# Loading three of four blocks of the near values again, in three transfers

## The chip, the cores and the metric

The kernel runs on one core of a Trainium2 chip. The metric is the device time of one execution in microseconds (us), the median of several runs.

## The reference, cut to what matters

```python
B, H, S, D = 4, 8, 768, 64             # block = 32, so 24 blocks of rows
scores = matmul(q, k.T) / sqrt(D)
mask = |blk_i - blk_j| <= 1            # neighbours
mask |= blk_i in (0, 23) or blk_j in (0, 23)     # end rows, end columns
mask |= blk_j in sampled_blocks[blk_i]           # three sampled blocks a row block
attn = softmax(where(mask, scores, -1e9))
x = matmul(attn, v)                    # (B, S, 512) after the heads are joined
# channel mix of x, shifted by one row
xk = mu_k * x + (1 - mu_k) * x_prev
xr = mu_r * x + (1 - mu_r) * x_prev
out = sigmoid(xr @ w_r) * (relu(xk @ w_k) ** 2 @ w_v)
```

A row block in the middle of a sequence sees eight key blocks: three sampled ones, its own with the two neighbours, and the two end blocks 0 and 23.

## The kernel before, in words

**Units.** The attention is done in 24 units: for each pair of batches one wide unit (the two end row blocks, which see all keys) and eleven near units of two neighbouring row blocks each (`UNITS`). Near unit m of a pair covers row blocks n = 2m+1 and n+1 for both batches, all eight heads. The matmuls of the channel mix are laid between those of the attention as their rows come ready.

**Buffers of near values.** For each of its two row blocks (j = 0, 1) a near unit needs two value buffers of 128 partitions by 4 KB (512 KB): one for the "far" side and one for the "near" side, each with four blocks of 32 rows. Partition k\*4+n holds row k of block n. The near side of j = 0 holds blocks [23, n-1, n, n+1], that of j = 1 holds [n, n+1, n+2, 23], so block 23 stands in the first place for j = 0 and in the last for j = 1, whatever the unit. The far side holds the three sampled blocks and block 0. There are eight buffers `VR[0..7]`: the first and second near units take four each, and from the third on `place_value` hands out `VR[0..3]` in turn, the same four for every unit: `VR[0]` and `VR[2]` for the far side, `VR[1]` and `VR[3]` for the near side. So a unit's values can be loaded only when the unit before has computed its value product.

**Loading.** `load_near` adds the loads of a unit to the plan. `close` (the near side) is one transfer of 512 KB of `vn`, in which the host has laid the four blocks in order. `gather` (the far side) is one transfer of 128 KB of `vt` for each sampled block, whose place is read from a register; block 0 is loaded only when the buffer doesn't hold it already (`slots` remembers for which pair it does). The keys of the near blocks come from `kd` (line 394) into the one key buffer `KR`, the queries from `qn` (line 379).

**Order.** All these transfers are issued by SP, one after the other. The order of all operations on every engine is written out by hand in `ORDER`; the numbers count the operations as they were added to the plan. `Plan.order` also bounds the bytes under way: an operation with transfers waits for the landing of the one that lies `QUEUED` = 2.2 million bytes back, counted with `wire` (bytes and a share for each row) by transfer (`parts` of an operation).

**What reads them.** `near_unit` computes scores (line 553; in the first three near units line 509) from `KR` and the queries, and the value product (line 583) from all four buffers of the unit: 128 matmuls in two groups of 64. The channel mix follows with r (line 773), h (line 793) and v (line 819). Its shifted and mixed inputs xk and xr are made in `split_x` (lines 739 to 752).

Of the kernel before, what the change touches and what calls it, by code (L numbers as in the profile page):

```python
# [25 lines left out]
QB, SLOTS = (4, 8)  # L26
# [4 lines left out]
SEEN = 5  # L31
DIRECT = 3
NEARBY = 0
COPIED = 4
FAR = 8000000000.0
ROOM = 32
# [4 lines left out]
def wire(size, row):  # L41
    return size * (1 + 195 / row)
# [109 lines left out]
def chosen(kind, i):  # L152
    return LETTER[PICK[kind][i]]
# [6 lines left out]
def block_sparse_attention_channel_mix(ctx: ExitStack, tc: tile.TileContext, kt, kd, kw, qw, qn, vt, vn, vw, blocks, own_near, mu_k, mu_r, w_k, w_v, w_r, out):  # L160
    nc = tc.nc
# [3 lines left out]
    plan = Plan()  # L165
    unit = WIDE_SCALE
    PE, ACT, DVE, POOL, SP = ('PE', 'ACT', 'DVE', 'POOL', 'SP')

    def buf(shape, dtype, tag, bufs, name, pool=sb):
        return Buf(pool, shape, dtype, tag, bufs, name)  # L170

    def fixed(shape, dtype, name):
        return Fixed(cp.tile(shape, dtype, name=name))

    def engine(on):
        return nc.scalar if on == ACT else nc.gpsimd if on == POOL else nc.vector

    def copy(on, to, of):
        if on == ACT:
            nc.scalar.copy(to, of)  # L180
        else:
            engine(on).tensor_copy(to, of)  # L182
# [6 lines left out]
    VR = [fixed([P, PAIR, DM], F32, f'VR{i}') for i in range(VR_BUFS)]  # L189
# [114 lines left out]
    slots = [None] * len(VR)  # L304
    turns = [0, 0]

    def place_value(kind):
        turns[kind] += 1
        first = len(VR) // 2
        return 2 * (turns[kind] - 1 if turns[kind] <= first else (turns[kind] - 1 - first) % (VR_BUFS // 2)) + kind  # L310

    def sampled_block(eng, pr, m, i):
        j, i = divmod(i, NRAND)
        n = PAIR * m + 1 + j
        if (eng.engine, n) not in sampled:
            _, (sampled[eng.engine, n],) = nc.values_load_multi_w_load_instructions(packed.ap[0:1, n:n + 1], engines=[eng.engine], min_val=0, max_val=ROOM ** NRAND - ROOM ** (NRAND - 1) * (ROOM - NB) - 1, skip_runtime_bounds_check_because='VectorE keeps each number within the blocks')
        if (eng.engine, pr, n, i) in sampled:
            return sampled[eng.engine, pr, n, i]
        at = sampled[eng.engine, n] >> 5 * i
        if i < NRAND - 1:  # L320
            kept = eng.alloc_register(f'block{pr}_{n}_{i}')
            eng.reg_alu(kept, at, ROOM - 1, ALU.bitwise_and)
            at = eng.snap(kept, min_val=0, max_val=NB - 1)
        else:
            at = nc.s_assert_within(at, 0, NB - 1, skip_runtime_bounds_check_because='VectorE keeps each number within the blocks')
        sampled[eng.engine, pr, n, i] = at
        return at
# [46 lines left out]
    def direct(pr, m):  # L374
        return pr == 0 and m < DIRECT

    def load_near(pr, m, i):
        q = buf([P, HP, P], F32, 'q', 2, f'q{pr}_{m}')
        plan.add(SP, lambda: nc.sync.dma_start(q.ap, qn[pr, m]), writes=[(q, *range(HP))], size=wire(262144, 2048))
        values = []  # L380
        n = PAIR * m + 1
        K = KR
        all_keys = whole[pr]
        by_block = lambda: all_keys.ap.rearrange('p h b (n x) -> p (h b) n x', x=BLK)
        if not m:

            def ends():
                for slot, end in ((END, 0), (WINDOW - 1, NB - 1), (2 * END + 1, 0), (WINDOW + 4, NB - 1)):
                    copy(POOL, K.ap[:, slot], by_block()[:, :, end])
            plan.add(POOL, ends, reads=[(all_keys, *EVERY)], writes=[(K, 'ends')])  # L390
        if pr == 0 and m < COPIED:
            plan.pick('near', m, lambda: copy(chosen('near', m), K.ap[:, WINDOW:WINDOW + 4], by_block()[:, :, n - 1:n + 3].rearrange('p a n x -> p n a x')), reads=[(all_keys, *EVERY)], writes=[(K, 'near')])
        else:
            plan.add(SP, lambda: nc.sync.dma_start(K.ap[:, WINDOW:WINDOW + 4].rearrange('p n a x -> p (n a x)'), kd[pr, :, n - 1:n + 3].rearrange('p n x -> p (n x)')), writes=[(K, 'near')], size=wire(524288, 4096))
        for j in range(PAIR if i in SENT else 0):

            def send(j=j):
                for r in range(NRAND):
                    at = sampled_block(nc.sync, pr, m, j * NRAND + r) + pr * NB
                    nc.sync.dma_start(K.ap[:, (NRAND + 1) * j + r].rearrange('p a x -> p (a x)'), kt[bass.ds(at, 1)].rearrange('o p x -> (o p) x'))  # L400
            plan.add(SP, send, reads=[(packed,)], writes=[(K, ('far', j))], size=wire(131072, 1024) * NRAND, parts=NRAND)
        for j in range(0 if i in SENT else PAIR):

            def fetch(j=j, key=PAIR * i + j):
                on = chosen('keys', key)
                eng = engine(on)
                for i in range(NRAND):
                    at = sampled_block(eng, pr, m, j * NRAND + i)
                    copy(on, K.ap[:, (NRAND + 1) * j + i], by_block()[:, :, bass.ds(at, 1)].rearrange('p a o x -> p a (o x)'))
            plan.pick('keys', PAIR * i + j, fetch, reads=[(packed,), (all_keys, *EVERY)], writes=[(K, ('far', j))])  # L410
        for j in range(PAIR):
            w = [place_value(0), place_value(1)]
            values.append(w)
            more = slots[w[0]] != pr
            slots[w[0]] = pr
            slots[w[1]] = None

            def close(w=w, j=j):
                nc.sync.dma_start(VR[w[1]].ap.rearrange('p b x -> p (b x)'), vn[pr, m, j])

            def gather(w=w, j=j, more=more):
                to = VR[w[0]].ap.rearrange('(k n) b x -> k n (b x)', n=QB)
                if more:
                    nc.sync.dma_start(to[:, NRAND], vt[pr * NB].rearrange('k b x -> k (b x)'))
                for i in range(NRAND):
                    nc.sync.dma_start(to[:, i], vt[bass.ds(sampled_block(nc.sync, pr, m, j * NRAND + i) + pr * NB, 1)].rearrange('o k b x -> (o k) (b x)'))  # L426
            plan.add(SP, close, writes=[(VR[w[1]], 0, 1)], size=wire(524288, 4096))
            plan.add(SP, gather, reads=[(packed,)], writes=[(VR[w[0]], 0, 1)], size=wire(131072, 4096) * (NRAND + more), parts=NRAND + more)
        return (q, K, values)

# [38 lines left out]
    def eight(keys, half, hp, j):  # L469
        i, b = (j % PAIR, j // PAIR)  # L470
        x = keys.ap[half, (NRAND + 1) * i:(NRAND + 2) * i + 1, PAIR * hp + b]
        block = PAIR * HP * BLK
        apart = (WINDOW - 1 + 2 * i - (NRAND + 1) * i) * block
        return replace(x, ap=[list(x.ap[0]), [apart, 2], [block, QB], [1, BLK]])
# [21 lines left out]
    def first_scores(pr, m, gi, s, q, keys):  # L496

        def mm():
# [3 lines left out]
            for a in range(2):  # L502
                hp = 2 * gi + a
                for j in range(QB):
                    i, b = (j % PAIR, j // PAIR)
                    for row, half in enumerate(HALF):
                        to = s.ap[ROWS[j], row, a * 256:(a + 1) * 256].rearrange('p (x r) -> p r x', r=SLOTS)
                        if not NEARBY:
                            nc.tensor.matmul(s.ap[ROWS[j], row, a * 256:(a + 1) * 256].rearrange('p (x g a) -> p g a x', g=2, a=QB), q.ap[half, hp, ROWS[j]], eight(keys, half, hp, j), start=False, stop=True, skip_group_check=True)
# [29 lines left out]
    def near_unit(b, m, together, carried, q, keys, values, o, L, t0, t1):  # L539
        scores, held = ([], [])  # L540
        for gi in range(2):
            s = buf([P, 2, 512], F32, 's', 2, f's{b}_{m}_{gi}', ps)
            if direct(b, m):
                plan.add(PE, first_scores(b, m, gi, s, q, keys), reads=[(q, 2 * gi, 2 * gi + 1), (keys, 'ends', ('far', 0), ('far', 1), *(() if NEARBY else ('near',))), (ident_16,), (first_mask,)] + [(whole[b], *EVERY)] * NEARBY, writes=[(s,)])
                scores.append(s)
# [350 lines left out]
    for op in plan.order():  # L896
        done = nc.cur_bb.bb.instructions
        n = len(done)
# [196 lines left out]
```

## Time and profile before

| | us |
|---|---|
| median of three runs | 527.81 |
| lowest and highest run | 527.33 and 532.04 |
| the profiled execution, its own time | 525.43 |
| its span (first to last instruction) | 523.7 |
| TensorE (PE) busy in the span | 506.4 |

Times in the rows below are microseconds from the start of the span. PE is TensorE's matmul, DVE VectorE, ACT ScalarE, POOL GpSimd; SP issues transfers, and "SPq" marks the issue of a transfer, not its flight. In the timeline a row is: start, time that it took, engine, line, operation, out<-in, count (a run of equal instructions is merged), and in brackets the engine's idle time before it and what ended it. The granted clock of TensorE is full in all 40 slices of the span.

### The profile page before, as it was taken

The numbers are of one execution on the slowest core, as the hardware profiler recorded it, in microseconds if no ns is written. First come the engines' busy times: TensorE is split into PE (matmuls) and PEld (weight loads), VectorE is DVE, ScalarE is ACT, GpSimd is POOL, SyncE is SP. The second block draws the span as 40 slices with busy tenths as digits, with TensorE's granted clock in tenths as the row PEclk, the third lists the DMA queues.
The fourth block names the chain that finished last, engine by engine and source line by source line (L and its number), as shares of the span: only waits on it lengthen the run. The fifth ranks groups of instructions, "written<-read, shape, count | busy, mean of one in ns | idle before, by whom it ended". The sixth has DMA issues, their size and how long they took to land.

```text
span 523.7 us, 17903 instructions
## 1 busy us (share of the span) xinstructions
PE 506.4 (97%) x7026; PEld 404.5 (77%) x7031; DVE 347.0 (66%) x841; ACT 309.1 (59%) x779; POOL 223.8 (43%) x288
## 2 busy tenths in 40 slices
PE   7889799999999999999999999999999999999997
PEld 2456578778878787677887888888988788888886
DVE  5899799986575775557767687675787536426401
ACT  2979898868746664365666467455675355343320
POOL 0634464433443635254063642353363444724530
PEclk9999999999999999999999999999999999999999
DMA  8999894663688887768977876877757414001002
GB/s 293 401 324 342 303 315 169 205 201 102 183 282 242 285 306 202 222 192 265 293 243 206 242 243 182 274 245 209 226 167 213 147 48 110 1 21 60 1 0 80
DMA packets 51765, 105.34 MB, mean 201 GB/s; under 512 B 7329, under 2 KB 27938, under 8 KB 51682
## 3 DMA queue, kind: packets, MB, share of 16 engines
q1 hardware_dynamic: 51394, 103.82, 62.3%
q8 instruction: 55, 0.90, 0.7%
q10 hardware_dynamic: 288, 0.39, 0.2%
q14 instruction: 28, 0.23, 0.1%
HBM read 80.07 MB, written 6.29 MB: 165 GB/s over the span
## 4 chain that ended last, share of the span: by engine, by line
PE 85%; DMA 7%; SPq 3%; DVE 3%; issue 1%; ACT 1%; ACTq 0%; DVEq 0%
PE v L819 25%; PE o L583 8%; PE s L553 7%; PE r_0p L773 5%; PE r_1p L773 5%; PE h_3p L793 5%; PE h_1p L793 4%; PE h_2p L793 4%; PE h_0p L793 4%; PE tx L643 2%; SPq L426 2%; DMA raw<-w_v 1%; PE sw L599 1%; PE t L461 1%; PE h_0p L805 1%
## 5 line engine op out<-in xcount | busy, mean ns | idle before, releaser
L819 PE MATMUL v<-w,k 128*128 128x512 f32 (+1 forms) x600 | 143.5, 390 | 0.0
L819 PEld LDWEIGHTS v<-w,k 128*128 128x128 f32 x600 | 107.8, 188 | 25.8 <-issue 1.4
L447 DVE CUSTOM_DVE_ANT_1 p<-s,near_mask 128x256 f32<-128x256 f32 x152 | 82.9, 628 | 27.4 <-DMA p<-tb 14.0
L452 ACT ACTIVATE p<-p,nm 128x256 f32<-128x256 f32 x152 | 76.1, 502 | 38.1 <-DVE nm L447 35.6
L182 POOL COPY KR<-keys 128x256 f32 (+2 forms) x72 | 30.3, 460 | 44.4 <-PE s L553 21.9
L479 DVE STREAM_TRANSPOSE tb<-p 128x1024 f32<-128x1024 f32 x30 | 37.2, 1240 | 12.4 <-ACT p L452 10.3
L822 DVE SCALAR_TENSOR_TENSOR z<-v,z 128x512 f32<-128x512 f32 (+1 forms) x25 | 16.4, 664 | 39.1 <-PE v L819 38.9
L553 PE MATMUL s<-KR,q 64*32 64x256 f32 x1216 | 38.7, 380 | 1.5 <-issue 1.4
L583 PEld LDWEIGHTS o<-VR,p 128*32 128x32 f32 x1920 | 28.0, 110 | 5.9 <-issue 3.3
L583 PE MATMUL o<-VR,p 128*32 128x64 f32 x1920 | 30.5, 220 | 0.8 <-PE r_0p L773 0.6
L553 PEld LDWEIGHTS s<-KR,q 64*32 64x32 f32 x1216 | 21.2, 106 | 12.7 <-issue 2.9
L773 PE MATMUL r_1p<-w,xr 128*128 128x512 f32 x120 | 30.3, 399 | 0.0
L773 PE MATMUL r_0p<-w,xr 128*128 128x512 f32 x120 | 30.2, 398 | 0.0
L452 ACT ACTIVATION_READ_ACCUMULATOR p<-p,nm 128x1 f32 x152 | 28.7, 189 | 0.0
L773 PEld LDWEIGHTS r_1p<-w,xr 128*128 128x128 f32 x120 | 22.1, 188 | 5.8 <-ACT xt L679 0.4
L773 PEld LDWEIGHTS r_0p<-w,xr 128*128 128x128 f32 x120 | 21.9, 188 | 4.7
L793 PE MATMUL h_3p<-xk,w 128*128 128x256 f32 x192 | 25.2, 285 | 0.0
L452 ACT ACTIVATE pw<-pw,nmw 128x768 f32<-128x768 f32 x16 | 14.9, 935 | 17.4 <-DVE nmw L447 10.0
L793 PE MATMUL h_2p<-xk,w 128*128 128x256 f32 x192 | 24.8, 285 | 0.0
L793 PEld LDWEIGHTS h_3p<-xk,w 128*128 128x128 f32 x192 | 23.5, 188 | 1.4 <-issue 0.8
L793 PEld LDWEIGHTS h_1p<-xk,w 128*128 128x128 f32 x192 | 23.3, 188 | 1.6 <-ACT pt L180 0.4
L793 PE MATMUL h_1p<-xk,w 128*128 128x256 f32 x192 | 24.4, 283 | 0.0
(226 smaller groups left out, 1048.0 us busy)
## 6 DMA issues: line engine op xcount, KB each, us to landing
VR<-vn SPq DMA_DIRECT2D x42, 512.0 KB, 4.9
VR<-vt SPq DMA_DIRECT2D x130, 128.0 KB, 3.3
p<-tb SPq DMA_DIRECT2D x120, 128.0 KB, 2.9
KR<-kd SPq DMA_DIRECT2D x18, 512.0 KB, 4.8
out<-z SPq DMA_DIRECT2D x23, 256.0 KB, 2.8
q<-qn SPq DMA_DIRECT2D x22, 256.0 KB, 5.2
keys<-kw SPq DMA_DIRECT2D x7, 768.0 KB, 7.5
raw<-w_k SPq DMA_DIRECT2D x4, 1024.0 KB, 8.0
```

Of the source, the lines that this page charges most:

```text
L182: engine(on).tensor_copy(to, of)
L426: nc.sync.dma_start(to[:, i], vt[bass.ds(sampled_block(nc.sync, pr, m, j * NRAND + i) + pr * NB, 1)].rearrange('o k b x -> (o k) (b x)'))
L447: nc.vector.tensor_tensor_reduce(out=dealt(p.ap[:, cs]), in0=cut(view()), in1=by, scale=-SCALE, scalar=3e+38 if first is None else nm.ap[: ...
L452: plan.add(ACT, lambda: nc.scalar.activation(p.ap[:, cs], p.ap[:, cs], AF.Exp, bias=nm.ap[:, col:col + 1], scale=-1.0, accum_out=L.ap[:, h ...
L479: plan.add(DVE, lambda: nc.vector.transpose(out=turned.ap.rearrange('p (k y c) -> p k y c', k=QB, c=BLK), in_=p.ap.rearrange('p (y k c) -> ...
L553: nc.tensor.matmul(s.ap[ROWS[j], row, a * 256:(a + 1) * 256].rearrange('p (x g a) -> p g a x' if carried else 'p (x a g) -> p g a x', g=2, ...
L583: nc.tensor.matmul(o.ap[ROWS[j], h * D:(h + 1) * D], held[gi][1](i, g, j), VR[values[j % PAIR][g]].ap[:, j // PAIR, h * D:(h + 1) * D], st ...
L643: nc.tensor.transpose(tp.ap[:, c, :], x.ap[:, c * P:(c + 1) * P], ident.ap)
L773: nc.tensor.matmul(pr.ap[:, 0:512], xr.ap[:, a, c, :], wr[c].ap[:, w, :], start=c == 0 and m == 0, stop=c == CC - 1 and m == 2)
L793: nc.tensor.matmul(ph.ap[:, ff * PAIR * TT:(ff + 1) * PAIR * TT], wk[f // 4 * CC + c].ap[:, w, f % 4 * P:(f % 4 + 1) * P], xk.ap[:, a, c, ...
L819: nc.tensor.matmul(pv.ap[:, 0:width], hid[f][2](a), wv[f].ap[:, w, cs], start=f == 0 and m == 0, stop=f == FC - 1 and m == 2)
L822: plan.add(DVE, lambda pv=pv, cs=cs: nc.vector.scalar_tensor_tensor(out=z.ap[:, cs], in0=pv.ap[:, 0:width], scalar=unit, in1=z.ap[:, cs], ...
```

## The change

For the third to seventh near unit of the first pair of batches (positions 3 to 7 in `UNITS`, below `ENDS_KEPT` = 8) `close` no longer loads block 23, which an earlier unit of the same pair has left in the same place of the same buffer. The other three blocks come as three transfers of 128 KB, each to every fourth partition, instead of one of 512 KB. `slots` now remembers for a near-side buffer the pair and j whose end block it holds. The counts for `QUEUED` follow. `ORDER` is the same; `close` stays one operation with three transfers issued one after another. The values that reach the product are the same.

```diff
+ENDS_KEPT = 8
...
             slots[w[0]] = pr
-            slots[w[1]] = None
-
-            def close(w=w, j=j):
-                nc.sync.dma_start(VR[w[1]].ap.rearrange('p b x -> p (b x)'), vn[pr, m, j])
+            kept = slots[w[1]] == (pr, j) and i < ENDS_KEPT
+            slots[w[1]] = (pr, j)
+
+            def close(w=w, j=j, kept=kept):
+                if not kept:
+                    nc.sync.dma_start(VR[w[1]].ap.rearrange('p b x -> p (b x)'), vn[pr, m, j])
+                    return
+                by_block = lambda x: x.rearrange('(k n) x -> k n x', n=QB)
+                for n in range(1 - j, QB - j):
+                    nc.sync.dma_start(by_block(VR[w[1]].ap.rearrange('p b x -> p (b x)'))[:, n], by_block(vn[pr, m, j])[:, n])
...
-            plan.add(SP, close, writes=[(VR[w[1]], 0, 1)], size=wire(524288, 4096))
+            plan.add(SP, close, writes=[(VR[w[1]], 0, 1)], size=wire(131072, 4096) * (QB - 1) if kept else wire(524288, 4096), parts=QB - 1 if kept else 1)
```

## Rows read from the trace of the kernel before

**Rows 1.** The page, part 4: the chain that ended last, by engine.

```profile
PE 85%; DMA 7%; SPq 3%; DVE 3%; issue 1%; ACT 1%; ACTq 0%; DVEq 0%
```

**Rows 2.** PE's waits: in total, times, longest (us).

```profile
PE o L583 <- DMA VR<-vn: 1.2, 1, 1.2
```

**Rows 3.** The chain that ended last, from 20 to 160: start, us.

```profile
63.63 5.67 DMA VR<-vn
```

**Rows 4.** Timeline of PE, 20 to 170.

```profile
69.35 1.88 PE L583 MATMUL o<-VR,pt 128*32 128x64 f32 x120 [1.23 <-DMA VR<-vn]
...
72.01 3.08 PE L793 MATMUL h_0p<-xk,w 128*128 128x256 f32 x24
...
75.45 1.09 PE L553 MATMUL s<-KR,q 64*32 64x256 f32 x32
...
83.99 1.10 PE L583 MATMUL o<-VR,pt 128*32 128x64 f32 x64
...
101.86 1.10 PE L583 MATMUL o<-VR,pt 128*32 128x64 f32 x64
102.89 1.09 PE L553 MATMUL s<-KR,q 64*32 64x256 f32 x32
...
118.04 1.10 PE L583 MATMUL o<-VR,pt 128*32 128x64 f32 x64
...
139.12 1.99 PE L583 MATMUL o<-VR,pt 128*32 128x64 f32 x128
```

**Rows 5.** Timeline of SP's issues, 20 to 170.

```profile
58.27 5.31 SPq L426 DMA_DIRECT2D VR<-vt  x6
63.63 1.10 SPq L419 DMA_DIRECT2D VR<-vn  x1
...
65.93 0.33 SPq L394 DMA_DIRECT2D KR<-kd  x1
...
75.51 1.99 SPq L426 DMA_DIRECT2D VR<-vt  x3
...
89.78 0.33 SPq L419 DMA_DIRECT2D VR<-vn  x1
...
92.78 5.00 SPq L426 DMA_DIRECT2D VR<-vt  x6
97.88 0.53 SPq L394 DMA_DIRECT2D KR<-kd  x1
...
111.22 1.98 SPq L426 DMA_DIRECT2D VR<-vt  x3
...
133.95 0.53 SPq L419 DMA_DIRECT2D VR<-vn  x1
134.57 0.38 SPq L823 DMA_DIRECT2D out<-z  x1
137.46 2.61 SPq L483 DMA_DIRECT2D p<-tb  x4
```

**Rows 6.** Line 426's instructions from 58.2 to 63.5: landing of its six transfers.

```profile
DMA to landing us min/median/max: 3.3/5.0/6.6
```

**Rows 7.** Timeline of POOL, 55 to 104.

```profile
69.84 1.30 POOL L752 TENSOR_TENSOR xk<-xk_0f,xk 128x512 fp32r<-128x512 f32 x1 [0.82 <-DVE xk L182]
```

**Rows 8.** Transfers issued at 65.93: count, size, us from issue to landing.

```profile
KR<-kd SPq DMA_DIRECT2D x1, 512.0 KB, 9.1
```

**Rows 9.** Line 424's instructions: time of an issue, ns, min/median/max.

```profile
L424 SPq DMA_DIRECT2D VR<-vt x4: 497/548/793, 25.3 to 241.0; - x4
```

**Rows 10.** SP's waits, 58 to 136.

```profile
SPq L419 <- PE o L583: 21.5, 4, 8.1
```

**Rows 11.** The transfer issued at 97.29.

```profile
VR<-vt SPq DMA_DIRECT2D x1, 128.0 KB, 2.5
```

**Rows 12.** The transfer issued at 97.88.

```profile
KR<-kd SPq DMA_DIRECT2D x1, 512.0 KB, 3.7
```

**Rows 13.** The transfer issued at 134.57.

```profile
out<-z SPq DMA_DIRECT2D x1, 256.0 KB, 4.2
```

## The prediction

> **What bounds the kernel now.** I read the page first. TensorE sets the time: four fifths and more of the chain that ended last is PE work, and transfers and SP's issuing together are a tenth of it [rows 1]. In the stretch of the third to seventh near unit the order on PE is fixed, so a transfer earns or costs only what it takes from or adds to a wait of PE. So I looked next for who waits for a near-value transfer. The list of PE's waits has one of 1.2 us for such a transfer, once [rows 2]. The timelines place it: the second close of the third unit is issued at 63.63 and lands 5.67 later, at 69.30 [rows 3], and the value product of the third unit goes on at 69.35 after 1.23 us of idle [rows 4]. The other four units show no idle time before their value products at 83.99, 101.86, 118.04 and 139.12 [rows 4]. There the question is how much room their transfers have, and for that I read SP's issues in time [rows 5], the landings of single transfers, and the PE instructions that need them.
>
> **How time counts.** The profiled run took 525.43 us, 523.7 of it span; the median of the runs shown is 527.81, that is 2.38 more. My sum is a difference on the profiled timeline, and I add it to the median.
>
> **What is removed.** Ten closes (two in each of five units) bring 384 KB instead of 512 KB, 1.25 MB less of 105. This matters only where PE waits for the queue. After the last gather of the third unit, which lands at about 66.4 (issued at 63.11, the last of the six that end at 58.27 + 5.31, landing 3.3 us after its issue [rows 5, 6]), the 512 KB close lands at 69.30. That is 2.9 us for 512 KB, or 0.72 for 128 KB. The new close has one block less, and the other close of the unit, ahead of it, too: by bytes it lands at 69.30 - 1.45 = 67.85. By issue it is later: the third piece leaves two issues after 63.63. At 0.6 us each (below), and at 1.1 where one is as long as the issue at 63.63 was [rows 5], that is 64.8 to 65.3, and with the 3.3 us of the last gather [rows 6] it lands at 68.1 to 68.6. PE would resume at 68.2 to 68.7 instead of 69.35, a gain of 0.65 to 1.15 us.
>
> What is late next? The h_0p product at 72.01 [rows 4] needs the shifted input whose last part GpSimd computes at 69.84 for 1.30 us, so to 71.14 [rows 7]; that does not hang on this wait. So h_0p can't start before about 71.2, and the gain there is at most 0.8. The scores of the fifth unit at 75.45 [rows 4] need a key transfer issued at 65.93 that lands 9.1 us later, at 75.0 [rows 5, 8]. It stands behind the two shortened closes, so by bytes it lands 1.45 earlier, at 73.6, and PE asks for it at 74.65; if its issue, 1.2 us later, counted in full instead, it would land at 76.2 and take all of the gain back. Its 9.1 us are mostly time behind other transfers, so I take the first. Gain of this stage: 0.8, between 0 and 0.8.
>
> **What is added: SP's time.** Each close is three issues where it was one. SP issues the gathers too, in the same order, so everything behind the closes is later. The trace has no three-piece close. The nearest rows are: an issue of one block of a fixed address, 0.50 to 0.79, median 0.55 [rows 9]; four carried transfers of fixed address in 2.61 us, 0.65 each with the gap [rows 5]; below, the 0.33 of the first issue after a wait [rows 5]; above, the 1.10 at 63.63. I take 0.6 for each added issue, nearest to the first two rows: 1.2 a close, 2.4 a unit, with 1.5 (0.38 each with its gap) and 3.0 (one of the four long) as ends. The fourth to seventh units start this row of issues only when the product of the unit before has freed the buffers (the list of SP's waits puts 21.5 us on it [rows 10]), so the 2.4 can't be laid ahead and is set against the room of each reader:
> - Fourth unit: the last gathers are issued by 77.50 and land by about 80.4; PE reads at 83.99 [rows 4, 5]. Room 3.5, and 1.1 is left.
> - Fifth unit: first close at 89.78, six gathers to 97.78, the last issued near 97.3 and landing 2.5 later, at 99.8; PE reads at 101.86 [rows 4, 5, 11]. Room 2.1: late by 0.3.
> - The keys of the seventh unit are queued behind those gathers: issued at 97.88, landing 3.7 later at 101.6; PE computes the scores with them at 102.89 [rows 4, 5, 12]. Room 1.3: late by 1.1. This is the tightest place, and the 0.3 just before is inside it.
> - Sixth unit: the gathers end at 113.20, so the last lands between 115.2 and 116; PE reads at 118.04 [rows 4, 5]. Room 2.0 to 2.8: nothing, or up to 0.4.
> - Seventh unit: its second close is the last, issued at 133.95; its landing is not shown, but the store issued right behind lands 4.2 after 134.57, at 138.8 [rows 13], so it lies between 137.5 (as quick as the key transfer above) and 138.8. PE reads at 139.12. Room 0.3 to 1.6. A 128 KB piece lands 1.2 sooner after its issue than 512 KB do (2.5 against 3.7 [rows 11, 12]), so 2.4 becomes 1.2: between 0.4 to spare and 0.9 late. I take 0.3 late.
>
> The Trainium skill (DMA: Bandwidth & Descriptors, section Issuing engines are not separate DMA queues) says that the time a sequencer takes to start a transfer is usually small beside the transfer. By it this whole term would be nil and the sum the gain alone, 527.0; here six issues take 5.31 us while a transfer lands in 2.5 to 3.7 when nothing stands before it, so the trace does not agree.
>
> Small edits together: the value product waits for three landings where it waited for one, two more for each of two buffers. No row prices a wait that is already met; the gap between SP's last gather (97.78) and the key transfer (97.88) bounds one at 0.1. They are taken while earlier matmuls run, so zero, up to 0.5 in all. The limit on bytes under way counts pieces of 128 KB instead of 512, so a wait for a landing can end only sooner: zero. The first close of the third unit stands ahead of the gathers at 58.27, and SP waits for PE between them; its two further issues are hidden there, and would cost at most 1.2 without that wait.
>
> **Sum.** -0.8 + 1.1 + 0.3 = +0.6 us: 526.0 for a run like the profiled one, 528.4 for the median. Against the 1% (5.3 us) that a measurement of this kernel can tell, given runs from 527.33 to 532.04, this is no change.
>
> **The rivals.**
> *The issues are hidden.* At 0.38 an added issue (1.5 a unit) the seventh unit's keys are late by 0.2, the close of the seventh has room, and 0.6 of the gain stays: 527.2. For it: the 0.33 issues. Against it: they are all first ones after a wait.
> *SP's issues become the bound of the fifth to seventh unit.* Place: keys at 102.89. It decides from room 1.3 plus gain 0.8 = 2.1 us for four issues, 0.53 each; above that the change is a loss. With one long issue in each unit, 3.0: keys 1.7 late, sixth unit up to 1.0 (take 0.5), seventh 0.9, less 0.8: +2.3, 530.1. For it: medians of 0.55 and 0.65 lie above the point already, and the 1.10 at 63.63 is one issue of seven in a row. Against it: fewer bytes let the keys land a little sooner.
> *The pieces land one after another, each with its own delay.* At 3.3 each a close takes 9.9: the third unit waits 4.2 more, the seventh reads at 133.95 + 1.2 + 9.9 = 145.0 instead of 139.12, 5.9 more: at least +10.1, 537.9. The six gathers speak against it: issued within 4.8 us, they land 6.6 (first) to 3.3 (last) after their issue, so within 1.6 us [rows 6]. The Trainium skill (the same page, section Rules for kernel authors) says that transfers to separate parts of the partitions serialize and should be one; these rows agree only as far as shared bandwidth goes.
> *Nothing is kept,* because the buffer's mark does not match: 527.8. The buffers alternate as the code shows, so I give it little.
>
> **How the numbers follow.** Forecast as summed (527.5 to 529.2) 0.45; hidden issues 0.22; SP as the bound 0.25; one after another 0.03; nothing kept 0.05. The range takes in hidden issues less the 0.5 by which the fastest run lies under the median, and SP as the bound with a little of the upward scatter: 526.4 to 531.0. All but one case lie within 1%; scatter and the wilder ends give 0.02 to faster and 0.06 to slower.
>
> **What would show it.** In the changed profile: 32 closes of 512 KB and 30 pieces of 128 KB; the idle time at the third unit's product down from 1.2 to under 0.5; a new PE wait of about 1 us for the keys before the seventh unit's scores, about 13 us after the fourth unit's product ends; a small one at the seventh unit's product. No new wait there means that the issues are cheaper than I think; waits at all four products that they are dearer. The prediction is wrong if the time moves by more than 3 us, which would need a wait of which these rows show nothing.

## The result and the profile after

The changed kernel takes 531.60 us (median of 22 runs, 527.50 to 537.75) where the kernel before took 527.79 beside it (median of 22, 525.25 to 532.04). The ratio is 1.0055, with an interval of 1.0032 to 1.0079: a loss of 2.9 us, between 1.7 and 4.2. (The ratio leaves out one run of the changed kernel in a slower state and is not the ratio of these two medians, which is 1.0072.) By the bound of the prediction that is within 1%, and 527.8 + 2.9 = 530.7 lies inside its range; the median of all runs lies 0.6 above it, and the interval of the loss reaches beyond the 3 us that the prediction named as its limit. The forecast was +0.6, so the sum is short by 2.3. The time came out near where the rival with SP's issues as the bound had put it, 530.1; the range held it because it took in that rival.

The profiled execution took 532.99 us, 531.2 of it span. The chain that ended last, by engine, from the page:

```profile
PE 79%; DMA 8%; SPq 5%; DVE 3%; ACT 2%; issue 2%; POOL 0%; ACTq 0%; DVEq 0%
```

Against [rows 1] PE gave up six points; SP's queue took two, transfers, ACT and "issue" one each. The end of the run still hangs on PE, but the chain now goes through SP more often. The transfers of the near side (count, size, us from issue to landing), for the whole kernel:

```profile
VR<-vn SPq DMA_DIRECT2D x32, 512.0 KB, 4.8
VR<-vn SPq DMA_DIRECT2D x30, 128.0 KB, 3.1
```

The 32 whole closes and 30 pieces are what the prediction asked for, so the rival in which nothing is kept is out. PE's waits for near-value transfers (us in total, times, longest), to be set against [rows 2]:

```profile
PE o L590 <- DMA VR<-vt: 1.9, 1, 1.9
...
PE o L590 <- DMA VR<-vn: 1.2, 2, 0.6
```

One wait for a close of 1.2 us has gone. In its place stand a wait of 1.9 for a gather and two of 0.6, one of which, at 45.6, lies ahead of the changed units. The timeline of PE shows the other two:

```profile
69.93 1.99 PE L590 MATMUL o<-VR,pt 128*32 128x64 f32 x128
...
84.98 1.10 PE L590 MATMUL o<-VR,pt 128*32 128x64 f32 x64
...
104.62 1.96 PE L590 MATMUL o<-VR,pt 128*32 128x64 f32 x64 [1.91 <-DMA VR<-vt]
106.50 1.96 PE L560 MATMUL s<-KR,q 64*32 64x256 f32 x32
...
122.61 1.39 PE L590 MATMUL o<-VR,pt 128*32 128x64 f32 x64
...
143.99 0.41 PE L590 MATMUL o<-VR,pt 128*32 128x64 f32 x10
...
145.04 1.88 PE L590 MATMUL o<-VR,pt 128*32 128x64 f32 x118 [0.64 <-DMA VR<-vn]
```

The third unit's product now runs in one piece, 128 matmuls without idle time, where [rows 4] had it split at 69.35. The fifth waits 1.91, the seventh is split after ten matmuls and waits 0.64. The fifth's product and the scores behind it take 1.96 each instead of 1.10 and 1.09: after its 1.91 us of idle, PE got half of its clock. Windows of the whole core (us, busy time and count of PE, its weight loads, VectorE, ScalarE and GpSimd, then the granted clock, DMA share and GB/s):

```profile
104.00:108.00 4.00, 3.38 (x96) 2.41 (x96) 2.37 (x5) 3.95 (x8) 1.66 (x3) 0.62 0.37 121
```

0.62 is the mean of a stretch that is partly at 2.4 GHz and mostly at 1.2. SP's issues in time show what holds the transfers up:

```profile
64.81 2.39 SPq L426 DMA_DIRECT2D VR<-vn  x3
...
71.97 1.76 SPq L426 DMA_DIRECT2D VR<-vn  x3
...
76.41 3.04 SPq L426 DMA_DIRECT2D VR<-vn  x3
80.05 2.00 SPq L433 DMA_DIRECT2D VR<-vt  x3
...
90.97 2.43 SPq L426 DMA_DIRECT2D VR<-vn  x3
...
94.06 1.74 SPq L426 DMA_DIRECT2D VR<-vn  x3
96.40 5.01 SPq L433 DMA_DIRECT2D VR<-vt  x6
101.51 0.53 SPq L395 DMA_DIRECT2D KR<-kd  x1
...
111.55 1.78 SPq L426 DMA_DIRECT2D VR<-vn  x3
...
118.45 2.00 SPq L433 DMA_DIRECT2D VR<-vt  x3
...
132.99 2.77 SPq L426 DMA_DIRECT2D VR<-vn  x3
...
140.99 1.81 SPq L426 DMA_DIRECT2D VR<-vn  x3
```

Of the kernel before, beside [rows 5], the starts of the first closes of the fourth, sixth and seventh unit and an issue inside the fifth:

```profile
71.28 0.33 SPq L419 DMA_DIRECT2D VR<-vn  x1
...
90.21 1.44 SPq L379 DMA_DIRECT2D q<-qn  x1
...
107.08 0.33 SPq L419 DMA_DIRECT2D VR<-vn  x1
...
128.12 0.33 SPq L419 DMA_DIRECT2D VR<-vn  x1
```

Read each unit from the start of its first close to the end of its last gather (of its last close in the seventh, which closes last). The fifth takes 90.97 to 101.41, 10.44 us, where [rows 5] give 89.78 to 97.78, 8.00: four added issues, 2.44 more. The sixth goes from 111.55 to 120.45, 2.78 more than before (8.90 against 6.12). The fourth and the seventh hold an issue that took over a us (three pieces in 3.04 and 2.77 instead of some 1.8) and are 3.86 and 3.45 longer (10.08 against 6.22, 9.81 against 6.36). The forecast was 2.4 a unit. The fifth's window holds a long issue in both kernels, the 1.44 for the queries before and one in the three pieces in 2.43 after, so its 2.44 is a difference with a long issue on either side.

The long issues have a companion in the traces. The profile names some queues "instruction". From 133.3 to 135.3, around the long issue of the seventh unit, one packet (count, MB, share) is on such a queue:

```profile
q8 instruction: 1, 0.02, 3.4%
```

From 111.5 to 120.5, where the sixth unit has no long issue, there is none. In the fourteen profiles together, 54 of SP's issues between 58 and 150 us took over 0.85 us, and 53 of them overlap such a packet; of the 995 shorter ones 161 do. That the packet holds the issue up is not shown by this. But a long issue is then no property of a piece: it stands in the kernel before as well, at 63.63 and 90.21, on other issues.

**One measure for all kernels.** The run starts at different moments in different profiles: the second unit's product comes up to 2.3 us later in most kernels, those that don't touch it included. The rest, from the end of the seventh unit's product to the end of the span, varies as well, from 382.6 to 389.3 us, though no kernel changes it. So I use two spans inside one profile. The *loss stretch* runs from the end of the third unit's product to the end of the seventh's: before 71.23 to 141.11, 69.88 us; after 71.92 to 146.92, 75.00. The *gain stretch* runs from the start of the scores of the fourth unit (62.10 in before, 64.24 in after) to the end of the third's product: 9.13 before, 7.68 after. In this one profile that is -1.45 + 5.12 = +3.7.

### The profile page after: what moved, and what is told of

It is laid out like the page before. It is cut to its first block, busy times and chain, and to the rows that moved or that the text cites. A ratio compares the mean times of both kernels' runs of the same rounds, so it can differ in the third digit from the quotient of the medians.

```text
span 531.2 us, 17932 instructions
## 1 busy us (share of the span) xinstructions
PE 511.1 (96%) x7031; PEld 407.5 (77%) x7031; DVE 344.1 (65%) x841; ACT 309.5 (58%) x779; POOL 225.3 (42%) x288
## 4 chain that ended last, share of the span: by engine, by line
PE 79%; DMA 8%; SPq 5%; DVE 3%; ACT 2%; issue 2%; POOL 0%; ACTq 0%; DVEq 0%
PE v L826 24%; PE o L590 8%; PE s L560 6%; PE h_1p L800 4%; PE h_2p L800 4%; PE r_0p L780 4%; PE h_3p L800 4%; PE h_0p L800 4%; PE r_1p L780 4%; PE tx L650 2%; DMA VR<-vt 2%; PE sw L606 2%; DVE pw L454 1%; DMA raw<-w_v 1%; SPq L433 1%
## 5 line engine op out<-in xcount | busy, mean ns | idle before, releaser
L183 POOL COPY KR<-keys 128x256 f32 (+2 forms) x72 | 31.8, 483 | 47.1 <-PE s L560 24.2
L560 PE MATMUL s<-KR,q 64*32 64x256 f32 x1216 | 39.8, 387 | 1.7 <-issue 1.6
L748 POOL TENSOR_TENSOR xr_0d<-xt 128x128 f32<-128x128 f32 x26 | 11.9, 471 | 29.9 <-DVE xr_0f L754 12.7
```

The lines of the kernel that those rows point to most:

```text
L748: engine(chosen('dif', k)).tensor_tensor(out=part(d.ap), in0=x.ap[:, two, c, 1:1 + TT], in1=x.ap[:, two, c, 0:TT], op=ALU.subtract)
```

## The experiments

The theory to be tested, called A in what was expected: the added issues on SP's queue delay the gathers, keys and last closes of the fourth to seventh unit, and that is the loss. Its rivals: the loss comes from the shorter or cut transfers of the third unit or from the start of the run; it comes from the sizes and landings, not from the issues; or it is the half clock behind the fifth's wait. All kernels below but the one with two small transfers start from the changed kernel. "Loss" and "gain" are the two stretches, against 69.88 and 9.13.

**Third unit alone, and the fourth to seventh alone.**

```diff
-            kept = slots[w[1]] == (pr, j) and i < ENDS_KEPT
+            kept = slots[w[1]] == (pr, j) and i == 3
```

> Only the third near unit keeps its end blocks. Theory A (SP's added issues make the fifth to seventh units late, and a long wait of PE there also halves TensorE's clock for some us): nothing is late any more, and the gain at the third unit's product is left, 0 to 0.8 us under before, ratio 0.9985 to 1.000. Theory B (the loss arises ahead of the third unit's product, where the changed kernel's profile has PE 2 us late and a first stretch of half clock at 57.2): as slow as the changed kernel, ratio 1.003 or more, with a granted clock under 1 in most runs.

Measured: 527.58 against 528.96, ratio 0.9965 (0.9935 to 0.9996), 1.85 us faster. Loss -0.3, gain -1.3. Of its timeline of PE, and then of GpSimd:

```profile
67.18 2.00 PE L590 MATMUL o<-VR,pt 128*32 128x64 f32 x128
...
69.95 3.08 PE L800 MATMUL h_0p<-xk,w 128*128 128x256 f32 x24
```

```profile
69.18 1.29 POOL L759 TENSOR_TENSOR xk<-xk_0f,xk 128x512 fp32r<-128x512 f32 x1 [0.82 <-DVE xk L183]
```

The h_0p product starts at 69.95, before GpSimd's operation ends at 70.47. By the loop in `hidden` (four chunks of three terms each, of which GpSimd writes the low part of the last two) its eighth matmul is the first that reads what GpSimd writes, and it runs at 70.86. So h_0p does need that operation, as I had thought, but only from its eighth matmul on, and here that one was not held up: the cap of 0.8 was too low.

```diff
-            kept = slots[w[1]] == (pr, j) and i < ENDS_KEPT
+            kept = slots[w[1]] == (pr, j) and 4 <= i < ENDS_KEPT
```

> Only the fourth to seventh near units keep their end blocks. Theory A: the loss of the changed kernel without the gain, ratio 1.006 to 1.008 (about +3 to +4 us), PE waits 1.5 to 2 us before the fifth unit's value product and 0.5 before the seventh's, granted clock half for some us behind the first. Theory B: within 1 us of before, ratio 0.999 to 1.002.

Measured: 533.37 against 528.96, ratio 1.0074 (1.0049 to 1.0100), 3.9 us slower. Loss +4.9, gain -0.2. The two halves of the change have opposite signs, and together they give -1.85 + 3.9 = +2.0, which agrees with the whole change's 2.9 within the intervals. Its PE, at the four places that the prediction named:

```profile
104.19 1.25 PE L590 MATMUL o<-VR,pt 128*32 128x64 f32 x64 [0.36 <-DMA VR<-vt]
...
106.64 1.10 PE L560 MATMUL s<-KR,q 64*32 64x256 f32 x32 [1.21 <-DMA KR<-kd]
...
123.10 1.24 PE L590 MATMUL o<-VR,pt 128*32 128x64 f32 x64 [1.24 <-issue]
...
145.50 1.88 PE L590 MATMUL o<-VR,pt 128*32 128x64 f32 x118 [0.80 <-issue]
```

Here the groups run at full clock, and the keys show as the wait of their own that was forecast. The two last waits have no releaser in the records ("issue"). The second splits the product after its tenth matmul, as a wait for a close does in the changed kernel.

**The same bytes in one transfer.** Where the change has three pieces, one transfer of 384 KB to the first 96 partitions.

```diff
-                for n in range(1 - j, QB - j):
-                    nc.sync.dma_start(by_block(VR[w[1]].ap.rearrange('p b x -> p (b x)'))[:, n], by_block(vn[pr, m, j])[:, n])
+                nc.sync.dma_start(VR[w[1]].ap.rearrange('p b x -> p (b x)')[0:96], vn[pr, m, j][0:96])
```

> The same 384 KB in all five units, but as one transfer into 96 partitions in a row (the blocks come to the wrong rows, so that values are wrong; the time is read alone). Theory A: SP has as many issues as before, so no product is late and the third unit's gain is left: ratio 0.9985 to 1.000, and no half clock behind the fifth unit. Theory B: if the fewer bytes themselves or the changed byte count bring the loss, 1.003 or more.

Measured: 528.96 against 528.96, ratio 1.0017 (0.9988 to 1.0045). Loss 0.0, gain +0.35. Of its PE:

```profile
103.51 1.10 PE L588 MATMUL o<-VR,pt 128*32 128x64 f32 x64
104.54 1.09 PE L558 MATMUL s<-KR,q 64*32 64x256 f32 x32
...
119.67 1.10 PE L588 MATMUL o<-VR,pt 128*32 128x64 f32 x64
...
140.70 1.99 PE L588 MATMUL o<-VR,pt 128*32 128x64 f32 x128
```

All the new waits are gone, with the same bytes as the change and the end block left out just so. So neither the kept block nor the smaller size makes the loss: it is the cutting into three, by its issues, its landings or its stride over the partitions, which this run does not tell apart. The third unit's product still waited 1.01 us in this profile, with less to bring.

**Four pieces.** Nothing is kept, and each close is four pieces: `range(QB)` instead of `range(1 - j, QB - j)`. That adds 30 issues where the change adds 20, and the bytes are those of before.

> The near side of the same five units comes as four transfers of one block, nothing is kept: the bytes of before, one issue more than the change. Theory A: 0.6 us more a close, 1.2 a unit beyond the change: fifth unit's product waits 3 us or more, sixth and seventh wait 1 to 2 each; ratio 1.010 to 1.016. Theory B: no more than the changed kernel, about 1.0055. If bytes mattered most, the third unit's wait would come back to 1.2 us or more with the fifth unit's unchanged.

Measured: 543.72 against 528.96, ratio 1.0253 (1.0203 to 1.0303), 13.4 us slower and far more than I had expected. Loss +14.2, gain -0.9. Of its PE:

```profile
106.94 1.25 PE L590 MATMUL o<-VR,pt 128*32 128x64 f32 x64 [2.73 <-DMA VR<-vt]
109.52 1.96 PE L560 MATMUL s<-KR,q 64*32 64x256 f32 x32 [1.33 <-DMA KR<-kd]
...
128.70 1.24 PE L590 MATMUL o<-VR,pt 128*32 128x64 f32 x64 [1.46 <-DMA VR<-vt]
...
153.24 3.24 PE L590 MATMUL o<-VR,pt 128*32 128x64 f32 x118 [2.40 <-DMA VR<-vn]
```

The same four places, each with more. For SP an issue costs what it did: the four units take 18.3 us more than before for 24 added issues, 0.76 each, where the change's 16 took 12.5, 0.78 each (measured as above). For PE the price is not a constant. The 5.7 us of further issuing make the loss stretch 9 to 11 us longer than in the changed kernel's two profiles: the change's issues are partly paid from the rooms, and behind the waits of 2.73 and 1.33 and of 2.40 PE ran groups at half clock (scores 1.96 instead of 1.09, the product 3.24 instead of 1.88; granted clock 0.55 from 108 to 112).

**Which unit.** In four kernels `i < ENDS_KEPT` becomes `i == 5` (fifth alone), `i in (3, 4)`, `i == 3` with four pieces, and `i == 3` with the one transfer of 384 KB.

> Only the fifth near unit keeps its end blocks, in three transfers. Theory A (SP's added issues eat the room of what is queued behind them): +1 to +2 us, ratio 1.002 to 1.004, with waits of PE of 1 to 2 us in all at the fifth unit's product and the seventh unit's scores, none at the sixth's and seventh's products. Rival (each of the four units pays the same, whatever its room): +0.7 to +1 us with a wait nowhere over 0.7 us.

Measured: 530.17 against 527.86, ratio 1.0031 (0.9989 to 1.0073), 1.6 us by its middle. Loss +1.8, gain 0.0. Of its PE:

```profile
103.95 1.25 PE L590 MATMUL o<-VR,pt 128*32 128x64 f32 x64 [0.46 <-DMA VR<-vt]
...
106.21 1.10 PE L560 MATMUL s<-KR,q 64*32 64x256 f32 x32 [1.01 <-DMA KR<-kd]
...
121.36 1.10 PE L590 MATMUL o<-VR,pt 128*32 128x64 f32 x64
...
142.43 1.99 PE L590 MATMUL o<-VR,pt 128*32 128x64 f32 x128
```

The interval of the time takes in no change, but the trace is plain: the fifth unit's pieces make the two waits forecast for them, 0.46 (forecast 0.3) and 1.01 (0.8), and none at the sixth and seventh.

> The third and the fourth unit keep their end blocks. Theory A: the fourth unit has 3.5 us of room against 2.4 us of added issues, so as with the third alone, 0.995 to 0.998, and no wait before the fourth unit's product. Rival (each unit pays the same): about 1 us slower than the third alone, 0.998 to 1.000.

Measured: 528.14 against 527.86, ratio 0.9983 (0.9945 to 1.0021). Loss +0.3, gain -1.4. The fourth's pieces cost little, as forecast; its product starts 0.3 later after the third's than in before, with no wait that the records show, and so it does with the third alone. The second half of its product, at 90.24, takes 1.50 instead of 1.10.

> Only the third near unit, its near side in four transfers of one block, nothing kept: the pieces without the saved bytes. If the gain of the third unit comes from the saved bytes (theory Bytes): ratio 1.000 to 1.002 and PE waits 1 us or more before the third unit's product. If it comes from the cutting into pieces (theory Pieces): 0.9965 to 0.9985 and a wait under 0.5 us.

Measured: 529.08 against 527.86, ratio 1.0009 (0.9979 to 1.0038). Loss +0.7, gain -1.3.

> Only the third near unit, its 384 KB as one transfer into 96 partitions in a row (blocks at wrong rows, so that values are wrong; the time is read alone): the saved bytes without the pieces. Theory Bytes: ratio 0.9955 to 0.998, wait before the third unit's product under 0.5 us. Theory Pieces: 0.999 to 1.002, wait of 1 us or more.

Measured: 527.11 against 527.86, ratio 1.0000 (0.9969 to 1.0031). Loss 0.0, gain -0.85. These two were to tell whether fewer bytes or the cutting shortens the third unit's wait. They don't: in its one profile each has the shorter gain stretch, and neither is measurably faster.

**Issues without bytes.** From the kernel before: two small transfers into memory that nobody reads, ahead of each whole close of the fourth to seventh unit.

The lines that keep the limit on bytes under way as it was are left out here.

```diff
             def close(w=w, j=j):
+                if 4 <= i < 8:
+                    for k in range(2):
+                        c = 2 * (4 * (i - 4) + 2 * j + k)
+                        nc.sync.dma_start(scratch.ap[0:32, c:c + 2], vn[pr, m, j, 0:32, 0:2])
                 nc.sync.dma_start(VR[w[1]].ap.rearrange('p b x -> p (b x)'), vn[pr, m, j])
```

> The kernel before, with two further transfers of 32 rows of 8 bytes into a buffer that nobody reads, ahead of each whole close of the fourth to seventh units: SP's issues of the change without its pieces, and without its saved bytes. Theory A (SP's issue time is the loss): about as with the fourth to seventh units changed, ratio 1.004 to 1.008, with waits at the fifth unit's product or the seventh's scores, and at the sixth's and seventh's products. Rival (three landings in place of one, or the way in which pieces land, is the loss): 0.999 to 1.002.

Measured: 527.48 against 527.91, ratio 0.9989 (0.9960 to 1.0019). Loss +0.2, gain -1.2. A miss: by theory A it should have been slower, and the time is where the rival had put it. SP's issues in the sixth unit show why it put no such burden on the queue:

```profile
108.28 0.35 SPq L424 DMA_DIRECT2D VR<-vn  x1
109.24 2.01 SPq L431 DMA_DIRECT2D VR<-vt  x3
111.30 1.04 SPq L423 DMA_DIRECT2D scratch<-vn  x2
112.38 0.42 SPq L424 DMA_DIRECT2D VR<-vn  x1
113.39 1.98 SPq L431 DMA_DIRECT2D VR<-vt  x3
```

The first close's two are missing here: they wait for no buffer, and SP had issued them at 101.30, in idle time. Only the second close's two lie between the first close and the last gather. The unit takes 7.09 us, 0.97 more than before; the change's takes 2.78 more. 0.97 (1.15 in the fifth) is less than every room but the smallest end of the seventh's, so PE does not see it. The kernel fits theory A with its rooms, but is no proof of it, and a kernel with the small transfers behind the release of the buffer was not run. For the fifth unit the traces settle part of it. PE waits there for the last gather and for the keys, which are not cut. With pieces in that unit the gather is issued 2.3 to 3.7 us later after the third unit's product than in before (four pieces: 6.0), and lands 2.3 to 2.7 us after its issue, as without pieces (3.5 once); the keys land 3.6 to 4.4 after theirs (4.9 once), against 3.7 to 4.2 without. So it is mainly their issue that is late, and not their landing.

The kernel shows one thing more: its third unit is that of before, and yet its product ran at 70.10 without a split, and its gain stretch is as short as with pieces. So the 1.2 us wait of [rows 2] is not in every execution: of the four profiles with that unit's close whole, it stands in three (1.23, 1.04 and 1.20).

**The clock.** Eight matmuls that nobody needs, ahead of the fifth unit's product, to keep PE busy while it waits.

```diff
+            if (b, m, gi) == (0, 4, 0):
+                one = nc.const_aps.tensor(1.0, (P, 512), BF16)
+                for k in range(8):
+                    nc.tensor.matmul(o.ap, one[:, 0:P], one, start=True, stop=True, skip_group_check=True)
```

> The changed kernel, with eight idle matmuls of 512 columns (1.7 us) ahead of the fifth unit's product, in the time in which PE waits there. If the half clock behind that wait is part of the loss: no half clock at 103 to 110 and 0.5 to 1.5 us faster than the changed kernel, ratio 1.002 to 1.0045. If it is not: 1.005 to 1.007, as the changed kernel.

Measured: 533.11 against 527.91, ratio 1.0106 (1.0069 to 1.0142), 5.6 us slower, so slower than the change itself. Of its PE:

```profile
103.49 1.91 PE L589 MATMUL o<-const-bfloat16-1.0 128*128 128x512 bf16 x8
105.33 1.10 PE L594 MATMUL o<-VR,pt 128*32 128x64 f32 x64
```

Both forecasts missed. The matmuls stand on PE behind no wait and are 1.91 us of work, but the loss stretch is +3.9, only 0.4 more than in the same kernel without them, below. Where the rest of the difference in time between the two arises is not shown: behind the seventh unit's product, where the two kernels are alike, this profile is 3.4 us longer than that one. No half clock follows; but there was none either in the kernel without them, profiled again:

> The changed kernel beside the others on one chip. Both theories: 1.003 to 1.008; theory A: waits of 1 us or more at the fifth unit's product or the seventh's scores, and under 1.3 us each at the sixth's and seventh's products.

Measured, with the changed kernel as it was: 531.54 against 527.91, ratio 1.0054 (1.0021 to 1.0088), the same loss again. Loss +3.5, gain -1.3. Of its PE:

```profile
93.06 0.42 PE L590 MATMUL o<-VR,pt 128*32 128x64 f32 x13 [1.26 <-issue]
...
105.62 1.25 PE L590 MATMUL o<-VR,pt 128*32 128x64 f32 x64 [0.40 <-DMA VR<-vt]
...
107.45 1.10 PE L560 MATMUL s<-KR,q 64*32 64x256 f32 x32 [0.58 <-DMA KR<-kd]
...
144.91 1.88 PE L590 MATMUL o<-VR,pt 128*32 128x64 f32 x118 [0.25 <-DMA VR<-vn]
```

The waits stand where they stood, smaller, and the two groups run at full clock. So the half clock at 104 is an event of the first profile, worth 0.86 + 0.87 = 1.7 us there, and no steady part of the loss. In its place stands an idle time of 1.26 us in the middle of the fourth unit's second product, whose buffers the first product had already read.

> The third unit alone, with five idle matmuls (1.1 us) ahead of the second unit's product, where PE waits 0.9 to 2.0 us in every profile and TensorE's clock is at half right after in some. If the half clock there costs what the rows show (3.4 us at half): 0.5 to 1 us faster than the third unit alone, ratio 0.994 to 0.997, and no half clock at 54 to 62. If not: 0.9965 to 0.999.

Here the kernel with the third unit alone got five such matmuls, `(0, 1, 0)` instead of `(0, 4, 0)`. They ran between the two halves of the second unit's product, at 58.89; they overwrite half of that product, so this part of the output is changed. Measured: 529.86 against 527.91, ratio 1.0024 (0.9999 to 1.0050). They ran behind the wait that they were to fill (2.06 here), at half clock (2.31 us for five), so the run says nothing on whether filling the wait would pay.

## Why the prediction was right or wrong

**Right: the direction of both parts, and the places.** The gain is at the third unit's product, the loss at the fifth's, the seventh's scores and the seventh's product, in that order, and the fourth has room for what its own product needs. The third unit alone is faster (by an interval that just excludes no change), the fourth to seventh alone are slower, and the same bytes in one transfer cost nothing.

**Right: the fifth unit's term.** Forecast 0.3 late at the product and 1.1 at the keys of the seventh, together 1.1. The waits of both places are 0.46 + 1.01 in the kernel with the fifth alone, 0.36 + 1.21 with the fourth to seventh, 0.40 + 0.58 in the changed kernel profiled again: 1.0 to 1.6. Its 2.4 us of added issuing were 2.44. That it is the forecast's 2.4 to the tenth is partly luck, as a long issue stands on either side of the difference. Only in the first profile of the change is it more, 1.91 at the product alone: the last of the six gathers was issued 0.65 later after the third unit's product there than with the fifth alone, and landed 3.5 us after its issue instead of 2.7.

**Mis-sized: the sixth and the seventh unit's products,** forecast 0 and 0.3. The price of the issues was taken as 2.4 for every unit, with 3.0 as the upper end, and the long issue as a rival. They took 2.78 in the sixth, and 3.86 in the fourth and 3.45 in the seventh, beyond that end. The sixth's product is 0.29 longer than before (1.39 against 1.10) in both profiles of the change, and waits 1.24 with the fourth to seventh alone; with four pieces it is a gather that it waits for. The seventh's product, from its first matmul to its last, takes 1.99 before, and 2.93 and 2.54 in the two profiles of the change and 3.10 with the fourth to seventh alone: 0.6 to 1.1 late instead of 0.3.

**Not in the sum at all:** the fourth unit's product, 0.2 to 0.5 later after the third's in the changed kernel's two profiles and in the fourth to seventh alone (0.25 also with the third alone, so not all of it is that unit's pieces); idle time with no releaser on PE, 1.26 at 93.06 in the repeated profile, 0.84 in the kernel of four pieces at the like place, 1.24 at the sixth's product with the fourth to seventh alone; and the half clock, 1.7 in one profile of two. Such idle time and half clock appear between 80 and 150 us in four of the five profiles with pieces in all of the fourth to seventh unit, and in none of the nine others, but for 0.1 us with the third and fourth unit changed. One place stands out: the second half of the fourth unit's product takes 0.4 to 1.6 us longer than its 1.10 in five of the six profiles with pieces in that unit, and 1.10 in all eight without. In the repeated profile the account closes: 0.2 (fourth) + 1.26 + 0.40 + 0.58 + 0.29 + 0.55 = 3.3 of 3.5. The forecast's places make 1.8 of that, the unnamed idle time the largest single part of the rest.

**Wrong: the cap on the gain.** I let h_0p wait for GpSimd's operation and so capped the gain at 0.8. h_0p starts before that operation ends, as its eighth matmul is the first to read the result, and the gain stretch is 1.2 to 1.45 shorter in every kernel with three pieces in the third unit. But it is 1.2 shorter with the two small transfers as well, where that unit is as before. As the wait is absent by itself in one of four profiles, its mean worth is less: I estimate 0.9, from 1.2 x 3/4. The timing of the third unit alone, 1.85 with 0.2 to 3.4 as ends, holds both.

**The rivals.** SP as the bound, to which I gave a quarter of the chance, is what happened: its deciding point was 0.53 us an issue, and the four units' 12.5 us for 16 issues are 0.78. Hidden issues: refuted by the fourth to seventh alone. Pieces that land one after another: refuted, as each of the third unit's last three lands 3.1 to 3.7 us after its own issue. I held the middle value because the median of one issue was the nearest row; the long ones come in four of the nine groups of three between 64 and 143 us (2.39 to 3.04 us instead of some 1.8), and the 1.10 at 63.63 had shown one, to which the prediction gave a price and too small a chance. The prediction also set six issues (5.31 us) against the landing of one transfer; one issue, about half a us, is small beside the 2.5 to 3.7 us of a landing. It is the adding up on one queue that costs, as the landings overlap and the issues don't.

The Trainium skill (DMA: Bandwidth & Descriptors, section Rules for kernel authors) advises one transfer in place of two to separate parts of the partitions. The runs agree with the advice, one transfer costing nothing where three cost 2.9 us; its reason, that such transfers serialize, is not what costs here, since each piece of the seventh unit's last close lands 2.5 to 2.7 us after its own issue, and it is the issues that come late.

**Open.** What the idle time without a releaser waits for. Whether the instruction packets make the long issues. Whether the landings of the pieces have a part in the loss at the sixth and seventh unit. Whether fewer bytes or the cutting shortens the third unit's wait. Whether the small loss of the gain with four pieces there is real. A version with only the third unit changed is the best of those run, 0.9965 of before; its interval just excludes no change, and four pieces or one transfer in the same place don't repeat it, so I would not count on more than a us.

## What to carry to other kernels

On a queue whose order is fixed and that starts on a buffer's release, fewer bytes bought with more issues pay only where PE waits for the last bytes: take the room of each later reader, and set the added issues against it unit by unit, with a long issue in most as the likely case and not as the worst. Keep such a change to the one place that shows a wait: the same edit was worth -1.85 us in the third unit and +3.9 in the four behind it. And before spending on a wait of a us, see whether it is in several profiles, as this one was only in three of the four that have that unit unchanged.

## What was not expected of the hardware

- Added issues cost SP alike and PE not: 20 of them make the kernel 2.9 us slower and 30 make it 13.4 slower, at 0.76 to 0.78 us of SP's time each in the fourth to seventh unit. With 20, waits of 0.3 to 1.9 us stand at the forecast's places; with 30 they are 1.3 to 2.7, and behind two of the places PE was at 1.2 GHz.
- SP's long issues go with packets on a queue that the profile calls "instruction": 53 of 54 overlap one.
- The length of a wait alone does not decide on PE's clock. At the second unit's product, which the change does not touch, PE waits 0.3 to 2.5 us; half clock followed 0.92 (fifth alone), 1.28 (third in four pieces), 1.63 (third and fourth), 2.00 (changed kernel, 0.65 granted from 56 to 60) and 1.83 to 2.46 in four more, and did not follow 0.33 (one transfer in all five), 1.14 (third alone), 1.35 (fourth to seventh), 1.44 (before), 1.52 (two small transfers) and 1.78 (third in one transfer).
- Transfers of 8 bytes to 32 partitions take SP nearly as long to issue as those of 128 KB: 1.04 us for two, against 1.76 to 1.81 for three.
